# A Fourier mixing layer and MLP: the first stage of two sequences in stacked form, and Silu in one pass

## Chip, core and metric

The kernel runs on one core of one Trainium2 chip. The metric is the device time of one execution in microseconds. The core's engines are named as in the profile: PE (TensorE matmul), PEld (its weight load), ACT (ScalarE), DVE (VectorE), POOL (GpSimd) and SP (SyncE, which here only issues DMAs).

## What is computed

`x` holds 4 sequences of 3008 tokens with 256 features. Each goes through a real Fourier transform over the tokens, a complex 256 x 256 product with a soft threshold, and the inverse transform; an MLP with 2048 hidden features and SiLU follows.

```python
X = rfft(x, axis=1)
Yr = Xr @ w_r - Xi @ w_i + b_r
Yi = Xr @ w_i + Xi @ w_r + b_i
Y = sign(Y) * maximum(abs(Y) - 0.01, 0)     # Yr and Yi apart
y = irfft(Y, n=3008, axis=1).reshape(12032, 256)
h = y @ w_in
out = (h / (1 + exp(-h))) @ w_out
```

## The kernel before

**The transform.** 3008 = 47 x 64: token t = 64 n2 + n1, with n2 below 47 and n1 = 32 h + j (h is 0 or 1, j below 32). The first stage ("s1") sums over n2 for 24 residues r, real and imaginary part: a product with a small table of cosines and sines. It writes to a scratch tensor in HBM (`scr1`). The second part works in 12 units `u` of two residues: `u_load` reads a unit back, `s2` or `s2_3` does the other DFT, `mix` or `mix3` the complex product, the threshold follows (in `mix3` as `shrink`, put off to the next tick), `i1` does the first inverse step and writes `scr2`. The last inverse step `i2` reads `scr2` through `g_load` and leaves y, transposed, in SBUF for the MLP.

**The MLP** goes through 24 blocks of 512 tokens (the last has 256) with 16 hidden slices `f` each, 376 pairs (i, f). One pair is a "tick". In tick t PE does `mlp1` of pair t (line 499, 6 matmuls of 512 columns), then what the tick has been given besides ("fill"), then `mlp2` of pair t-2 (lines 539 and 543). Between them ACT takes the sigmoid of h from PSUM (line 506), DVE multiplies it by h (line 507); one tick later `split_g` rounds g to the part gh on ACT (line 516) and leaves the rest gl to DVE (line 517).

**Split numbers.** A matmul in fp32r rounds its operands, so a value goes in as a high part and a rest, and a product is high x high + high x rest + rest x high: three matmuls (`s1_product`, line 173).

**What sets the order.** The code is written out tick by tick; each engine runs its own instructions in that order. Sequence 0 is transformed ahead of the ticks (prologue), with part of sequence 1's first stage and the split of the first MLP weights. `fill` holds the rest: `at` puts a call in a tick, `put` in the next tick that is not taken. `W_GO` says how many steps of the weights' split (`w64_split`, lines 599 to 613, on ACT and DVE in turn) go into ticks 0 to 22. `mix3_weights` makes wi - wr and wi + wr and their splits with POOL (lines 315 and 319). `x_ahead` issues the next load of x on POOL's queue (line 158, 94 rows of 4 KB). Stores go through a list that `flush` issues on SP's queue.

**First stage of sequences 2 and 3** (b = 2, 3). A group g of 4 token columns (of 8) is a tile of 94 rows, (n2, h). `s1_split` rounds one half of it, 512 columns, on ACT (line 218) and subtracts on DVE (line 219); in a later tick `s1_half` multiplies (line 173, three matmuls), copies the result on ACT and splits the other half. That is 16 halves a sequence and 3 matmuls a half.

**End of the prologue** (lines 738 to 763). The last `i1` of sequence 0 stores to `scr2` through ACT's queue (line 138). `g_load` of groups 0 and 1 for rows 0 to 87, a store of sequence 1's first stage (`flush(1)`), and `g_load` for rows 88 to 95, which waits for that last store, follow on SP; then `i2(0, 0)` can run. Block 0 needs columns j = 0 to 5, that is group 0 and the first half of group 1.

Of the kernel before, what the change touches and what calls it, by code (L numbers as in the profile page):

```python
# [37 lines left out]
def dft_tables():  # L38

    n1 = np.arange(KK)  # L40
    n2 = np.arange(RR)
    r = np.arange(NR)
    k = np.arange(KK)

    def trig(num, den):
        num = np.mod(num, den)
        c, s = np.cos(2 * np.pi * num / den), np.sin(2 * np.pi * num / den)
        s = np.where(2 * num % den == 0, 0.0, s)
        return c, s
# [48 lines left out]


@with_exitstack  # L100
def spectral_mlp_kernel(ctx: ExitStack, tc: tile.TileContext, x, w_r, w_i, b_r, b_i, w_in, w_out, c1, c2, c3, c4, c3f, out):
    nc = tc.nc
    cst = ctx.enter_context(tc.tile_pool(name="cst", bufs=1))
    sb = ctx.enter_context(tc.tile_pool(name="sb", bufs=2))
# [18 lines left out]
    def bank(name):  # L123

        tag, bufs = "d", 2
        if state["prologue"]:
            state["d"] = (state["d"] + 1) % 4
            tag, bufs = (("d", 2), ("acc", 4), ("h", 2), ("acc", 4))[state["d"]]
        return ps.tile([128, 512], F32, tag=tag, bufs=bufs, name=name)
# [28 lines left out]
            nc.gpsimd.dma_start(out=t[:NP, :], in_=v)  # L158
        return t

    x_next = [(b, g) for b in range(NB) for g in range(8)]

    def x_ahead():
        if x_next:
            q = x_next.pop(0)
            x_t[q] = x_load(*q)

    x_t = {}
    x_pre = []
# [42 lines left out]
            store(v[:, g * 4 * D:(g + 1) * 4 * D], o)  # L212
            del x_t[1, g], x_t[1, g, "o"]

    def s1_split(b, g, i):
        t = x_t[b, g][:NP, i * 512:(i + 1) * 512]
        sx = sb.tile([128, 2, 512], F32R, tag="sx", bufs=1, name="sx")
        nc.scalar.copy(sx[:NP, 0, :], t)
        nc.vector.tensor_sub(sx[:NP, 1, :], t, sx[:NP, 0, :])  # L219
        x_t[b, g, i] = sx  # L220

    def s1_half(b, g, i):
        sx = x_t.pop((b, g, i))
        if i == 0:
            x_t[b, g, "o"] = sb.tile([128, 4 * D], F32, tag="s1o", bufs=2, name="s1o")[:96, :]
        o = x_t[b, g, "o"]
        p = bank("s1")
        s1_product(p, (sx[:, 0, :], sx[:, 1, :]))
        nc.scalar.copy(o[:, i * 512:(i + 1) * 512], p[:96, :])
        if i == 0:  # L230
            s1_split(b, g, 1)
        else:
            v = scr1[b].rearrange("r (a j) d -> (r a) (j d)", a=4)
            store(v[:, g * 4 * D:(g + 1) * 4 * D], o)
            del x_t[b, g], x_t[b, g, "o"]
            x_ahead()
# [68 lines left out]
    def mix3_weights():  # L305
        t = sb.tile([128, 2, 2 * D], F32, tag="s1o", bufs=2, name="w32")
        nc.sync.dma_start(out=t[:, :, 0:D], in_=w_r.rearrange("(e p) d -> p e d", p=128))
        nc.sync.dma_start(out=t[:, :, D:2 * D], in_=w_i.rearrange("(e p) d -> p e d", p=128))
        for i, v in enumerate((b_r, b_i)):
            nc.sync.dma_start(out=bias[:, i, :], in_=v.unsqueeze(0).to_broadcast([128, D]))  # L310
        yield
        ds = []
        for op in (ALU.subtract, ALU.add):
            ds.append(sb.tile([128, 2, D], F32, tag="i1o", bufs=2, name="w32d"))
            nc.gpsimd.tensor_tensor(out=ds[-1], in0=t[:, :, D:2 * D], in1=t[:, :, 0:D], op=op)
        yield
        for d, dst in zip(ds, (wi, ws)):
            nc.scalar.copy(dst[0], d)
            nc.gpsimd.tensor_sub(dst[1], d, dst[0])

    def s2_3(b, u):
        a, t2 = u_t[b, u]
# [83 lines left out]

    g_t = {}

    def g_load(b, g, rows=slice(0, 96)):

        if (b, g) not in g_t:
            g_t[b, g] = sb.tile([96, 4 * D], F32, tag="gin", bufs=4, name="gin")
        v = scr2[b].rearrange("r (a j) d -> (r a) (j d)", a=4)
        nc.sync.dma_start(out=g_t[b, g][rows, :], in_=v[rows, g * 4 * D:(g + 1) * 4 * D])

    def pieces(c0, n):

# [74 lines left out]
    def mlp1(i, f):  # L492
        n = BLOCKS[i][1]
        h, l = xt[i]
        p = ps.tile([128, 512], F32, tag="h", bufs=2, name="h")
        m = 0
        for e in range(2):
            for w, v in ((win[0], h), (win[1], h), (win[0], l)):
                nc.tensor.matmul(  # L499
                    out=p[:, :n], lhsT=w[:, e, f * 128:(f + 1) * 128], rhs=v[:, e, :n],  # L500
                    start=(m == 0), stop=(m == 5),
                )
                m += 1
# [111 lines left out]
    with tc.manual_schedule():  # L615
        first = sb.tile([128, 1], F32, tag="rest", bufs=1, name="first")
        nc.gpsimd.memset(first, 0.0)
        nc.scalar.activation(out=first, in_=first, func=ACTF.Sigmoid)
        zero = sb.tile([128, 512], F32, tag="c", bufs=1, name="zero")
        x_sb.append(sb.tile([128, 4 * D], F32, tag="sx", bufs=1, name="x_sb2"))  # L620
        x_pre.extend(x_sb)
# [127 lines left out]
        w_go()
        w_tags[:] = [(("zl", 2), ("zh", 2))]  # L750
# [107 lines left out]
```

## Time and profile before

| | |
|---|---|
| runs | 1384.2 us median of 3 (1383.86 to 1386.02) |
| profiled execution | 1384.09 us, span of its instructions 1382.2 us |
| busy | PE 1362.8 us (99%), PEld 1166.1 (84%), DVE 887.7 (64%), ACT 704.8 (51%), POOL 98.6 (7%) |
| mean granted TensorE clock | 0.997 |
| DMA | 103.51 MB, 75 GB/s over the span |

A busy share counts an engine's instructions from start to end, and matmuls overlap, so 99% on PE says that it seldom sat without one, not that it ran at its peak. The chain that ended last goes back from the last instruction to what released it. The timeline shows single instructions, with the wait ahead of one and its releaser in brackets.

### The profile page before, as it was taken

The numbers are of one execution on the slowest core, as the hardware profiler recorded it, in microseconds if no ns is written. First come the engines' busy times: TensorE is split into PE (matmuls) and PEld (weight loads), VectorE is DVE, ScalarE is ACT, GpSimd is POOL, SyncE is SP. The second block draws the span as 40 slices with busy tenths as digits, with TensorE's granted clock in tenths as the row PEclk, the third lists the DMA queues.
The fourth block names the chain that finished last, engine by engine and source line by source line (L and its number), as shares of the span: only waits on it lengthen the run. The fifth ranks groups of instructions, "written<-read, shape, count | busy, mean of one in ns | idle before, by whom it ended". The sixth has DMA issues, their size and how long they took to land.

```text
span 1382.2 us, 20362 instructions
## 1 busy us (share of the span) xinstructions
PE 1362.8 (99%) x7621; PEld 1166.1 (84%) x7621; DVE 887.7 (64%) x1517; ACT 704.8 (51%) x1386; POOL 98.6 (7%) x145
## 2 busy tenths in 40 slices
PE   8989999999999999999999999999999999999998
PEld 4967788888888888888888888888888888888888
DVE  3858969687655677767655577776654555455555
ACT  5545455555564555555454445454454444444444
POOL 2000012111100101111100011111000000000000
PEclk9999999999999999999999999999999999999999
DMA  8865314231423213333121022220210110011001
GB/s 283 260 214 157 113 55 119 70 102 32 121 77 102 58 42 107 86 98 80 47 76 53 21 77 59 76 81 24 61 29 15 27 39 10 18 27 39 0 16 24
DMA packets 69939, 103.51 MB, mean 75 GB/s; under 512 B 7313, under 2 KB 53009, under 8 KB 69841
## 3 DMA queue, kind: packets, MB, share of 16 engines
q1 hardware_dynamic: 58169, 79.07, 19.6%
q0 software_dynamic: 8096, 19.45, 5.2%
q10 hardware_dynamic: 3575, 3.70, 0.9%
q8 instruction: 60, 0.98, 0.3%
q14 instruction: 39, 0.31, 0.1%
HBM read 64.70 MB, written 37.49 MB: 74 GB/s over the span
## 4 chain that ended last, share of the span: by engine, by line
PE 92%; DVE 3%; DMA 2%; ACT 1%; issue 1%; SPq 0%; DVEq 0%; ACTq 0%
PE h L499 36%; PE acc L539 24%; PE acc L543 12%; PE mix L352 5%; PE i L442 3%; PE mix L291 2%; PE s L327 2%; PE i L400 2%; PE s L173 2%; PE acc L534 1%; DMA scr<-s1o 1%; PE i L397 1%; PE s L270 1%; PE i2e L442 1%; DVE gl L517 1%
## 5 line engine op out<-in xcount | busy, mean ns | idle before, releaser
L499 PE MATMUL h<-xt,win 128*128 128x512 f32 (+1 forms) x2304 | 584.8, 389 | 0.0
L539 PE MATMUL acc<-wout,gh 128*128 128x512 f32 x1472 | 540.4, 401 | 0.7 <-ACT gh L516 0.7
L499 PEld LDWEIGHTS h<-xt,win 128*128 128x128 f32 x2304 | 400.9, 188 | 82.2 <-DVE xt L459 0.4
L506 ACT ACTIVATE g<-h 128x512 f32<-128x512 f32 (+1 forms) x385 | 226.4, 588 | 378.4 <-PE h L499 377.4
L543 PE MATMUL acc<-wout,gl 128*128 128x256 f32 x1472 | 412.8, 280 | 3.4 <-DVE gl L517 3.3
L507 DVE TENSOR_TENSOR g<-h,g 128x512 f32<-128x512 f32 (+1 forms) x385 | 261.2, 678 | 236.7 <-ACT g L506 233.0
L517 DVE TENSOR_TENSOR gl<-g,gh 128x512 fp32r<-128x512 f32 (+1 forms) x385 | 276.4, 718 | 172.5 <-ACT gh L516 167.3
L539 PEld LDWEIGHTS acc<-wout,gh 128*128 128x128 f32 x1472 | 276.9, 188 | 61.6 <-ACT gh L516 2.4
L516 ACT CAST gh<-g 128x512 fp32r<-128x512 f32 (+1 forms) x385 | 235.1, 611 | 155.2 <-DVE g L507 152.7
L543 PEld LDWEIGHTS acc<-wout,gl 128*128 128x128 f32 x1472 | 278.0, 189 | 15.2 <-DVE gl L517 6.0
L359 POOL TENSOR_TENSOR q<-q,bias 128x256 f32<-128x256 f32 x36 | 26.4, 733 | 652.5 <-ACT q L358 652.5
L442 PEld LDWEIGHTS i<-c_sb,gin 96*128 96x128 f32 x420 | 55.5, 195 | 11.3 <-issue 5.8
L372 DVE TENSOR_TENSOR y<-q,mix 64x256 f32<-64x256 f32 x144 | 60.3, 419 | 2.2
L442 PE MATMUL i<-c_sb,gin 96*128 96x94 f32 x420 | 54.7, 275 | 5.6 <-DMA gin<-scr 5.6
L327 PEld LDWEIGHTS s<-t,a 128*128 128x128 f32 x288 | 37.7, 191 | 3.0
L327 PE MATMUL s<-t,a 128*128 128x128 f32 x288 | 37.9, 274 | 0.0
L459 DVE TENSOR_TENSOR xt<-i,xt 128x376 fp32r<-128x376 f32 (+2 forms) x48 | 28.0, 584 | 14.7 <-ACT xt L458 14.7
L173 PE MATMUL s<-sx,c 94*96 94x512 f32 (+1 forms) x111 | 34.1, 414 | 0.3 <-DVE sx L219 0.3
L458 ACT CAST xt<-i 128x376 fp32r<-128x376 f32 (+2 forms) x48 | 24.2, 503 | 19.9 <-PE i L442 19.9
L400 PE MATMUL i<-zh,t 128*128 128x256 f32 x144 | 33.7, 297 | 0.0
L404 ACT COPY i1o<-i 128x512 f32<-128x512 f32 x48 | 27.9, 581 | 9.5 <-PE i L397 8.2
L560 DVE TENSOR_TENSOR o<-acc,o 128x256 f32<-128x256 f32 x92 | 32.6, 414 | 0.0
(119 smaller groups left out, 1168.8 us busy)
## 6 DMA issues: line engine op xcount, KB each, us to landing
a<-scr SPq DMA_DIRECT2D x48, 256.0 KB
gin<-scr SPq DMA_DIRECT2D x30, 384.0 KB
scr<-s1o SPq DMA_DIRECT2D x29, 384.0 KB
t<-in_c_dram POOLq DMA_DIRECT2D x36, 256.0 KB, 3.0
scr<-i1o SPq DMA_DIRECT2D x36, 256.0 KB
x_sb<-in_x_dram POOLq DMA_DIRECT2D x22, 376.0 KB, 4.2
t<-in_c_dram SPq DMA_DIRECT2D x48, 128.0 KB
w<-in_moe_w_in_dram SPq DMA_DIRECT2D x8, 512.0 KB
```

What stands on the lines that cost most here:

```text
L173: nc.tensor.matmul(out=p[:96, :], lhsT=c1_hl[m][:K, :], rhs=hl[k][:K, :], start=(n == 0), stop=(n == 2))
L327: nc.tensor.matmul(out=pv[:, e, :, r, :], lhsT=a[:, r, e * 128:(e + 1) * 128], rhs=t2[:, r * 128:(r + 1) * 128], start=True, stop=True,)
L352: nc.tensor.matmul(out=out, lhsT=x_[:, e, c, :], rhs=m[:, e, :], start=(n == 0), stop=(n == 5))
L400: nc.tensor.matmul(out=pv[:, r, :], lhsT=t3[:, m, q], rhs=z[k][:, r, :], start=(n == 0), stop=(n == 2),)
L442: nc.tensor.matmul(out=p[:, o:o + m], lhsT=g_t[b, j // 4][:, q:q + 128], rhs=c4_sb[:, p0:p0 + m], start=True, stop=True,)
L499: nc.tensor.matmul(out=p[:, :n], lhsT=w[:, e, f * 128:(f + 1) * 128], rhs=v[:, e, :n], start=(m == 0), stop=(m == 5),)
L506: nc.scalar.activation(out=g[:, q], in_=p[:, q], func=ACTF.Sigmoid)
L507: nc.vector.tensor_tensor(out=g[:, q], in0=p[:, q], in1=g[:, q], op=ALU.mult)
L516: nc.scalar.copy(gh[:, q], g[:, q])
L517: nc.vector.tensor_sub(gl[:, q], g[:, q], gh[:, q])
L539: nc.tensor.matmul(out=a, lhsT=gh[:, q], rhs=wout[:, f].rearrange("p a c -> p (a c)"), start=begins, stop=False,)
L543: nc.tensor.matmul(out=a[:, D:2 * D], lhsT=gl[:, q], rhs=wout[:, f, 0, :], start=False, stop=ends,)
```

## The change

Four things change.

1. *First stage of sequences 2 and 3, stacked.* A piece q (16 a sequence) takes one half h of n1 and 4 columns j. `x_load_twice` loads its 47 rows of 1024 columns twice, to partitions 0 to 46 and 64 to 110 of one tile (two DMAs on POOL's queue). `stack_split` rounds all 111 partitions in one ACT pass and turns the second copy into the rest on DVE. A new table `c5` holds the high part of the cosines and sines in 64 output columns and the rest in the other 64. `stack_product` then needs one matmul for 512 columns, two a piece; ACT copies the lower output half out of PSUM and DVE adds the upper one. The product comes two ticks after the split, not one.
2. *Silu in one ACT pass* in place of Sigmoid on ACT and a multiply on DVE.
3. *`mix3_weights` on DVE* instead of POOL, its last two steps in ticks 22 and 23 instead of 19 and 22.
4. *End of the prologue*: only the first half of group 1 is loaded ahead of `i2(0, 0)`; its other half, and the first-stage store, follow behind the loads of rows 88 to 95.

The ticks of the first stage and of the units of sequences 2 and 3 move with it.

```diff
+    c, s = trig(np.outer(n2, r), RR)
+    c5 = np.zeros((128, 2, KK))
+    c5[:RR, 0, :2 * NR] = np.stack([c, -s], axis=2).reshape(RR, 2 * NR)
...
+    c5[:RR, 1] = c5[:RR, 0] - c5h
+    c5[:RR, 0] = c5h
+    c5[64:64 + RR] = c5[:RR]
...
+    def x_load_twice(b, q):
+        t = x_sb[q % 2]
+        if b == STACKED and q < 2:
+            nc.gpsimd.memset(t[32:64, :], 0.0)
+        h, g = divmod(q, 8)
+        v = x[b].rearrange("(n h j) d -> n h (j d)", h=2, j=NJ)[:, h, g * 4 * D:(g + 1) * 4 * D]
+        for p in (0, 64):
+            nc.gpsimd.dma_start(out=t[p:p + RR, :], in_=v)
+        return t
...
-    def s1_split(b, g, i):
...
-    def s1_half(b, g, i):
...
+    def stack_split(b, q):
+        t = x_t[b, q]
+        sx = sb.tile([128, 4 * D], F32R, tag="sx", bufs=1, name="sx")
+        nc.scalar.copy(sx[:64 + RR, :], t[:64 + RR, :])
+        nc.vector.tensor_sub(sx[64:64 + RR, :], t[64:64 + RR, :], sx[64:64 + RR, :])
+        x_t[b, q] = sx
+
+    def stack_product(b, q):
+        sx = x_t.pop((b, q))
+        o = sb.tile([128, 4 * D], F32, tag="s1o", bufs=2, name="s1o")[:2 * NR, :]
+        for i in range(2):
+            p = bank("s1")
+            c = slice(i * 512, (i + 1) * 512)
+            nc.tensor.matmul(out=p, lhsT=c5_sb[:64 + RR, :], rhs=sx[:64 + RR, c], start=True, stop=True)
+            nc.scalar.copy(o[:, c], p[64:64 + 2 * NR, :])
+            nc.vector.tensor_tensor(out=o[:, c], in0=p[:2 * NR, :], in1=o[:, c], op=ALU.add)
...
+        x_ahead()
...
-            nc.gpsimd.tensor_tensor(out=ds[-1], in0=t[:, :, D:2 * D], in1=t[:, :, 0:D], op=op)
+            nc.vector.tensor_tensor(out=ds[-1], in0=t[:, :, D:2 * D], in1=t[:, :, 0:D], op=op)
...
-            nc.gpsimd.tensor_sub(dst[1], d, dst[0])
+            nc.vector.tensor_sub(dst[1], d, dst[0])
...
-            nc.scalar.activation(out=g[:, q], in_=p[:, q], func=ACTF.Sigmoid)
-            nc.vector.tensor_tensor(out=g[:, q], in0=p[:, q], in1=g[:, q], op=ALU.mult)
+            nc.scalar.activation(out=g[:, q], in_=p[:, q], func=ACTF.Silu)
...
+        urgent = (slice(0, 4 * D), slice(0, 2 * D))
         for g in range(2):
             loaded.add((0, g))
-            g_load(0, g, slice(0, 88))
-        flush(1)
+            g_load(0, g, slice(0, 88), urgent[g])
         u_step(NU + 1)
         s1(1, 3, late=True)
         for g in range(2):
-            g_load(0, g, slice(88, 96))
+            g_load(0, g, slice(88, 96), urgent[g])
+        flush(1)
+        g_load(0, 1, cols=slice(2 * D, 4 * D))
...
-        for t in (16, 19, 22):
+        for t in (16, 22, 23):
             at(t, next, m3, None)
...
-        for b, t0, dt in ((1, t + 11, 3.1), (2, 92, 5), (3, 186, 5)):
+        for b, t0, dt in ((1, t + 11, 3.1), (2, 104, 4.3), (3, 190, 4.8)):
...
-        for b, t0, dt in ((2, 37, 6), (3, 110, 8)):
+        for b, t0, dt in ((2, 54, 2.8), (3, 114, 4.4)):
             t = 0
-            for g in range(8):
-                t = max(t, t0 + dt * g)
-                at(t, s1_split, b, g, 0)
-                t = put(t + 1, s1_half, b, g, 0)
-                t = put(t + 1, s1_half, b, g, 1)
+            for q in range(16):
+                t = max(t, int(t0 + dt * q))
+                at(t, stack_split, b, q)
+                t = put(t + 2, stack_product, b, q)
```

**Where instructions move.** PE, in sequence 2's first stage, around one product (`s` is a PSUM bank, `c` the table, `sx` the split x). Before, one half:

```order
L499 MATMUL h<-xt_3309,win_79 128x512
L173 MATMUL s_3936<-sx,c_0_67 96x512 x2
L173 MATMUL s_3936<-sx,c_1_68 96x512
L539 MATMUL acc<-wout,gh 128x512
L543 MATMUL acc<-wout,gl 128x256
```

Now, one piece:

```order
L523 MATMUL h<-xt_3230,win_80 128x512
L254 MATMUL s_3974<-sx,c_sb 128x512
L254 MATMUL s_3978<-sx,c_sb 128x512
L562 MATMUL acc<-wout,gh 128x512
L566 MATMUL acc<-wout,gl 128x256
```

Three matmuls a half become two a piece, on another table.

ACT in the same stage, from one product to the next thing it copies out, before:

```order
L229 COPY s1o<-s_3775 96x512
L218 CAST sx<-x_sb_70 94x512
L516 CAST gh<-g 128x512
L506 ACTIVATE g<-h 128x512
L229 COPY s1o<-s_3808 96x512
```

And now:

```order
L255 COPY s1o<-s_3844 48x512
L255 COPY s1o<-s_3848 48x512
L244 CAST sx<-x_sb_70 111x1024
L539 CAST gh<-g 128x512
L530 ACTIVATE g<-h 128x512
L482 CAST xt_3813<-i_3879 128x376
```

A tick with a product holds two copies of 48 x 512 and a split of 111 x 1024, and the next tick none of them.

SP at the end of the prologue (`gin` is what `g_load` fills, `scr1_1` takes the first stage of sequence 1). Before:

```order
L414 DMA gin_967<-scr2_0_86 88x1024
L414 DMA gin_969<-scr2_0_86 88x1024
L142 DMA scr1_1_83<-s1o_960 96x1024
L414 DMA gin_967<-scr2_0_86 8x1024
L414 DMA gin_969<-scr2_0_86 8x1024
L583 DMA w64_999<-in_moe_w_out_dram 128x2x512
```

And now:

```order
L438 DMA gin_968<-scr2_0_87 88x1024
L438 DMA gin_970<-scr2_0_87 88x512
L438 DMA gin_968<-scr2_0_87 8x1024
L438 DMA gin_970<-scr2_0_87 8x512
L157 DMA scr1_1_84<-s1o_961 96x1024
L438 DMA gin_970<-scr2_0_87 96x512
L606 DMA w64_1001<-in_moe_w_out_dram 128x2x512
```

The store stood ahead of the loads of the last 8 rows and stands behind them; the second load is half as wide.

DVE during the split of the weights (`ww` and `we`), ticks 2 to 4, before:

```order
L601 TENSOR_SCALAR ww<-ww 128x512
L602 SCALAR_TENSOR_TENSOR ww<-w_1055,ww 128x512
L517 TENSOR_TENSOR gl<-g,gh 128x512
L507 TENSOR_TENSOR g<-h,g 128x512
L459 TENSOR_TENSOR xt_1090<-i_1150,xt_1089 128x376
L608 TENSOR_SCALAR we<-ww 128x512
L609 SCALAR_TENSOR_TENSOR we<-w_1055,we 128x512
L612 TENSOR_TENSOR ww<-ww,win_79 128x512
L613 TENSOR_TENSOR win_80<-ww,we 128x512
```

And now:

```order
L624 TENSOR_SCALAR ww<-ww 128x512
L625 SCALAR_TENSOR_TENSOR ww<-w_1057,ww 128x512
L540 TENSOR_TENSOR gl<-g,gh 128x512
L483 TENSOR_TENSOR xt_1090<-i_1148,xt_1089 128x376
L631 TENSOR_SCALAR we<-ww 128x512
L632 SCALAR_TENSOR_TENSOR we<-w_1057,we 128x512
L635 TENSOR_TENSOR ww<-ww,win_80 128x512
L636 TENSOR_TENSOR win_81<-ww,we 128x512
```

The multiply `g<-h,g` is gone from between gl and the weights' steps.

## Rows read from the trace of the kernel before

**Rows 1.** Page, part 4: the chain that ended last, by engine.

```profile
PE 92%; DVE 3%; DMA 2%; ACT 1%; issue 1%; SPq 0%; DVEq 0%; ACTq 0%
```

**Rows 2.** Stretches: length, busy PE, PEld, DVE, ACT, POOL, clock, DMA share, GB/s.

```profile
80.00:100.00 20.00, 15.31 (x68) 10.21 (x67) 9.83 (x17) 8.40 (x15) 0.00 (x0) 0.92 0.63 205
...
160.00:180.00 20.00, 17.52 (x83) 13.73 (x84) 18.39 (x29) 9.78 (x19) 1.23 (x2) 1.00 0.30 86
...
400.00:500.00 100.00, 100.00 (x552) 85.98 (x550) 61.26 (x104) 51.44 (x99) 6.10 (x10) 1.00 0.24 71
```

**Rows 3.** Chain in order (start us, us, what), two pairs of ticks.

```profile
176.39 1.39 PE h L499 x6
179.17 1.39 PE h L499 x6
...
399.35 1.39 PE h L499 x6
402.83 1.39 PE h L499 x6
```

**Rows 4.** Groups by shape: busy us, mean ns, idle before, its releasers.

```profile
L507 DVE TENSOR_TENSOR g<-h,g 128x512 f32<-128x512 f32 x368 | 254.3, 691 | 234.1 <-ACT g L506 231.9
...
L506 ACT ACTIVATE g<-h 128x512 f32<-128x512 f32 x368 | 220.0, 598 | 374.9 <-PE h L499 374.6
...
L219 DVE TENSOR_TENSOR sx<-x_sb,sx 94x512 fp32r<-94x512 f32 x32 | 22.4, 699 | 10.0 <-ACT sx L218 9.9
...
L608 DVE TENSOR_SCALAR we<-ww 128x512 uint32<-128x512 uint32 x16 | 7.8, 487 | 0.3
```

**Rows 5.** Timeline 88 to 104 us: start us, us, what, wait.

```profile
88.03 0.72 SPq L414 DMA_DIRECT2D gin<-scr  x2
...
88.45 0.41 ACTq L138 DMA_DIRECT2D scr<-i1o  x1
...
88.84 0.31 SPq L142 DMA_DIRECT2D scr<-s1o  x1
...
95.50 0.60 SPq L414 DMA_DIRECT2D gin<-scr  x2
...
97.64 2.42 PE L442 MATMUL i<-c_sb,gin 96*128 96x94 f32 x10 [4.69 <-DMA gin<-scr]
...
103.80 1.25 PE L442 MATMUL i<-c_sb,gin 96*128 96x94 f32 x10
```

**Rows 6.** Short stretches, columns as in rows 2.

```profile
30.00:32.00 2.00, 0.98 (x9) 1.01 (x10) 0.69 (x1) 0.97 (x3) 0.00 (x0) 1.00 0.97 289
...
96.00:97.00 1.00, 0.00 (x0) 0.00 (x0) 0.00 (x0) 0.00 (x0) 0.00 (x0) 0.85 0.24 66
...
103.00:104.00 1.00, 1.00 (x5) 0.54 (x3) 0.10 (x1) 0.25 (x1) 0.00 (x0) 0.74 0.00 0
```

**Rows 7.** Timeline of ticks 0 to 24, columns as in rows 5.

```profile
104.83 3.42 PE L499 MATMUL h<-xt,win 128*128 128x512 f32 x12
...
109.64 0.68 PE L442 MATMUL i<-c_sb,gin 96*128 96x94 f32 x4 [0.96 <-DMA gin<-scr]
...
125.87 1.02 PE L208 MATMUL s<-x_sb,c_sb 128*96 128x512 f32 x2
...
158.28 2.71 POOL L315 TENSOR_TENSOR w32d<-w 128x512 f32<-128x512 f32 x2 [26.92 <-DMA w<-in_w_i_dram]
...
158.45 1.42 DVE L608 TENSOR_SCALAR we<-ww 128x512 uint32<-128x512 uint32 x1
...
162.20 0.38 PE L543 MATMUL acc<-wout,gl 128*128 128x256 f32 x1 [1.50 <-DVE gl L517]
...
181.78 1.55 PE L499 MATMUL h<-xt,win 128*128 128x512 f32 x6
```

**Rows 8.** Line 158's transfers; the stretch 8 to 10 us as in rows 2.

```profile
DMA to landing us min/median/max: 3.4/4.5/9.5
...
8.00:10.00 2.00, 1.67 (x5) 0.73 (x5) 0.00 (x0) 1.02 (x2) 0.52 (x1) 1.00 1.02 272
```

More of the change, by code (lines that the diff above doesn't have):

```diff
@@ L32 @@
 S1_SPLIT = (3, 4, 5, 6, 7)
+STACKED = 2
 X_BUFS = [0, 1, 2, 3, 4, 5, 6, 0, 1, 2, 3, 4, 0, 2, 1, 0]
@@ L90, in dft_tables @@
     c3f = c3
+    c, s = trig(np.outer(n2, r), RR)
+    c5 = np.zeros((128, 2, KK))
+    c5[:RR, 0, :2 * NR] = np.stack([c, -s], axis=2).reshape(RR, 2 * NR)
+    c5[:, :, 1] = 0.0
+    c5 = c5.astype(np.float32)
+    bits = c5[:RR, 0].view(np.uint32).astype(np.uint64)
+    c5h = ((bits + 0x7FF + ((bits >> 12) & 1)) & 0xFFFFF000).astype(np.uint32).view(np.float32)
+    c5[:RR, 1] = c5[:RR, 0] - c5h
+    c5[:RR, 0] = c5h
+    c5[64:64 + RR] = c5[:RR]
     return {
@@ L96, in dft_tables, with spectral_mlp_kernel @@
         "c3f": c3f,
+        "c5": c5.reshape(128, 128),
     }
 @with_exitstack
-def spectral_mlp_kernel(ctx: ExitStack, tc: tile.TileContext, x, w_r, w_i, b_r, b_i, w_in, w_out, c1, c2, c3, c4, c3f, out):
+def spectral_mlp_kernel(ctx: ExitStack, tc: tile.TileContext, x, w_r, w_i, b_r, b_i, w_in, w_out, c1, c2, c3, c4, c3f, c5, out):
     nc = tc.nc
@@ L111, in spectral_mlp_kernel @@
     c4_sb = cst.tile([96, NP], F32, name="c4_sb")
+    c5_sb = cst.tile([128, 128], F32R, name="c5_sb")
     bias = cst.tile([128, 2, D], F32, name="bias")
@@ L159, in x_load @@
         return t
-    x_next = [(b, g) for b in range(NB) for g in range(8)]
+    def x_load_twice(b, q):
[7 more added lines that the diff above has]
+        return t
+    x_next = [(b, g) for b in range(NB) for g in range(16 if b >= STACKED else 8)]
     def x_ahead():
@@ L165, in x_ahead @@
             q = x_next.pop(0)
-            x_t[q] = x_load(*q)
+            x_t[q] = (x_load_twice if q[0] >= STACKED else x_load)(*q)
     x_t = {}
@@ L213, in s1_later @@
             del x_t[1, g], x_t[1, g, "o"]
-    def s1_split(b, g, i):
[L216 to L220, printed above, removed]
-    def s1_half(b, g, i):
[L223 to L236, printed above, removed]
+    def stack_split(b, q):
[13 more added lines that the diff above has]
+            nc.vector.tensor_tensor(out=o[:, c], in0=p[:2 * NR, :], in1=o[:, c], op=ALU.add)
+        h, g = divmod(q, 8)
+        v = scr1[b].rearrange("r (i h j) d -> (r i) h (j d)", i=2, h=2)
+        store(v[:, h, g * 4 * D:(g + 1) * 4 * D], o)
+        x_ahead()
     u_t = {}
@@ L407, in spectral_mlp_kernel, with g_load @@
     g_t = {}
-    def g_load(b, g, rows=slice(0, 96)):
+    def g_load(b, g, rows=slice(0, 96), cols=slice(0, 4 * D)):
         if (b, g) not in g_t:
             g_t[b, g] = sb.tile([96, 4 * D], F32, tag="gin", bufs=4, name="gin")
-        v = scr2[b].rearrange("r (a j) d -> (r a) (j d)", a=4)
-        nc.sync.dma_start(out=g_t[b, g][rows, :], in_=v[rows, g * 4 * D:(g + 1) * 4 * D])
+        v = scr2[b].rearrange("r (a j) d -> (r a) (j d)", a=4)[:, g * 4 * D:(g + 1) * 4 * D]
+        nc.sync.dma_start(out=g_t[b, g][rows, cols], in_=v[rows, cols])
     def pieces(c0, n):
@@ L617, in spectral_mlp_kernel @@
         nc.gpsimd.memset(first, 0.0)
-        nc.scalar.activation(out=first, in_=first, func=ACTF.Sigmoid)
+        nc.scalar.activation(out=first, in_=first, func=ACTF.Silu)
         zero = sb.tile([128, 512], F32, tag="c", bufs=1, name="zero")
@@ L796, in spectral_mlp_kernel @@
             at(t, x_ahead)
+        at(30, nc.gpsimd.dma_start, c5_sb, c5)
         m3 = mix3_weights()
-        for t in (16, 19, 22):
+        for t in (16, 22, 23):
             at(t, next, m3, None)
         t = 13
-        for b, t0, dt in ((1, t + 11, 3.1), (2, 92, 5), (3, 186, 5)):
+        for b, t0, dt in ((1, t + 11, 3.1), (2, 104, 4.3), (3, 190, 4.8)):
             at(t0 - 2, u_load, b, 0)
```

## Prediction

> **What bounds the kernel now.** I read the chain that ended last first, because it says which engine the end hangs on: PE holds 92% of it [rows 1]. Next come the stretches, which say where PE does not run: from 400 to 500 us it is busy for all 100, with DVE at 61 and ACT at 51; from 80 to 100 us it is busy for 15.31 of 20, from 160 to 180 us for 17.52 [rows 2]. In the second of these DVE is busy for 18.39 of 20, which 400 to 500 us is far from. So outside the first 182 us only less work on PE shortens the kernel; inside them there are waits to win. Last I read starts of ticks, since "busy" also counts a matmul that stands and waits: a plain tick lasts 179.17 - 176.39 = 2.78 us, a tick with a first-stage half 402.83 - 399.35 = 3.48 [rows 3]. Six matmuls of 512 columns take 1.39 us there, 0.232 each.
>
> **The sum** is made against the profiled execution, 1384.1 us; the median of the runs is 1384.2, so I add nothing for that.
>
> *Stacked first stage.* Removed are 32 halves of 0.70 us (3.48 - 2.78), 22.4 us. Added are 64 matmuls of 512 columns. No row has one of 111 rows and 128 output columns; the first MLP layer with 128 and 128 takes 0.232, the old half with 94 and 96 took 0.70 / 3 = 0.233 [rows 3], so size between these does not matter: 64 x 0.232 = 14.8 us. Term: **-7.6 us**, all on the path, since PE does not wait in that stage.
>
> Around it ACT and DVE get more for a piece. On ACT: two copies of 48 x 512 and a split of 111 x 1024. On DVE: two adds and a subtraction of 47 x 1024. Copies cost about the 0.60 of an ACT pass over 512 columns, adds 0.69 to 0.70 [rows 4]; the 1024 wide ones cost at most twice the 512 wide, 1.2 and 1.4. A tick with a product then asks ACT for its usual two passes and 2.4 us more, 3.6, against 2.78 + 0.46 = 3.24 on PE, and its neighbour without one for 1.2 against 2.78: 4.8 of 6.0 in two ticks. DVE gets 2.8 more a piece and loses 0.69 a tick. What PE needs in a tick was rounded in the tick before, so a late ACT in one of two has over a us to make it good: nothing on the path. If that cover is gone, see the third rival.
>
> On POOL's queue 64 loads of 47 rows take the place of 16 of 94, on SP's 32 stores of half the size that of 16; the bytes read for x double. The old loads land in 4.5 us (median) [rows 8]. A buffer is free once its split is done (1.2 + 1.4 us), then the next load is issued (two DMAs, about 0.5 us apart) and must land before the split two pieces on: 2.6 + 0.5 + 4.5 = 7.6 us in a time of four ticks and four matmuls, 12.0 us. So 4.4 us of slack, and nothing on the path.
>
> For these loads a rule of the Trainium skill speaks against the change. The page "DMA: Bandwidth & Descriptors", section "Why a DMA increments its semaphore by 16 and not by 1", says that a DMA runs on the largest number of engines, up to 16, that divides its row count, which leaves 47 rows one engine and 94 rows two; it knows an exception, some POOL-issued copies that get ceil(rows / 16) rows an engine on 16. Rows 8 disagree with the rule and agree with the exception: 385 kB in 4.5 us is 86 GB/s, and two engines at the 17 GB/s that one moves in the stretch shown (272 / 16) would need 11.3 us. By the rule the sum would be that of the last rival.
>
> *End of the prologue.* PE stands for 4.69 us until `gin` lands at 97.64. The loads of the last 8 rows leave SP at 95.50, 7.05 us after the store that they wait for, at 88.45 [rows 5]. In its way on the DMA engines are two loads of 88 rows, 704 KB, and, issued at 88.84, a store of 384 KB; with its own 256 KB that is 1376 kB in 7.05 us, 195 GB/s, and the stretch has 205 [rows 2]. So it waits for bytes. Now 352 + 176 + 256 KB = 803 kB stand there, 4.1 us. If the order counts more than the bytes, only the 176 KB go, 0.9 us. Ends: -0.9 and -2.9; I take -2.2, as the three share the engines to the end. Term: **-2.2 us**. Late next is the store itself, issued some 5 us later, whose buffer a later first-stage copy of the prologue needs; several steps of PE lie between.
>
> *Clock.* The granted clock fell to 1.2 GHz at about 96.7 (0.85 in that us), after 3.7 us without a matmul, and was back at 2.4 GHz at about 103.5 (0.74 in that us); where PE was idle half the time, at 30 to 32 us, it stayed at 1.00 [rows 6]. An idle time of 2.5 us lies between; I take the clock to stay, as the fall came well after that much. Ten `i2` matmuls took 2.42 us at the low level and 1.25 at the high one [rows 5]; PE worked 5.9 us at the low level, so 2.9 us come back at most and 0 at least. Some of that turns into waits on ACT: **-2.0 us**.
>
> *Silu, and POOL's work on DVE.* From the first `mlp1` at 104.83 to tick 24 at 181.78 [rows 7] are 76.95 us. Work for PE in it: 24 ticks x 2.78 = 66.7, less 2.8 (two ticks have no `mlp2`), plus 20 `i2` matmuls at 0.125, 2.5, plus two late first-stage products of 1.02 [rows 5, 7]: 68.4. So 8.5 us are waits. 1.0 is for `gin` [rows 7] and stays. 1.9 come with POOL's two passes at 158.28: beside them line 608 takes 1.42 us where its mean is 0.49 [rows 4, 7], and the next DVE step is as late again; PE then waits 1.50 for gl. With this work on DVE they go; four passes of 0.69 come to DVE in ticks 22 and 23, which is not full there. The other 5.6 come from DVE's order: the multiply (0.69 us) stands ahead of the weights' steps, waits for the sigmoid, and ACT waits for those steps before it rounds the next g. Without it DVE falls from 18.39 to about 13.5 of 20 us. I take two thirds, 3.7. An ACT pass with Silu is not in the trace; it lies between the 0.60 of Sigmoid [rows 4] and that plus the multiply, and I take 0.60, the same engine and tile. The new order has a single load of a function table, as before. Ends: -1.9 and -7.5. Term: **-5.6 us**. In the remaining 1200 us 254 us of DVE work go and buy nothing, since PE is busy there throughout.
>
> *Ticks of units and pieces moved.* The same work on PE in other ticks; sequence 2's units end by tick 164 where its first block is loaded at 167, sequence 3's by 258 for 263. Nothing.
>
> Sum: -7.6 - 2.2 - 2.0 - 5.6 = -17.4, so 1366.7; **I say 1366.5 us**, its own range 1361 to 1370.
>
> **Rivals.**
> - *The prologue keeps its gap* (14%): the store's 7 us are its own latency, and the clock falls as before. Against it speaks 195 GB/s beside 205. 4.2 us less: 1370.7.
> - *The weights still hold ticks 0 to 23* (10%): ACT and DVE take turns over the weights as before, and only POOL's 1.9 us come back. For it: the steps wait for each other, not only for the multiply. 1370.4.
> - *Both product banks in one tick* (11%): a product now takes both rotating PSUM banks at once, and waits for the pass that reads the older one, or ACT is late with its 3.6 us. At 0.25 us a tick in 32 ticks it is 8 us: 1374.5; at 0.55, as much as the 17 us won, it is no change. Against it: two ticks lie between products.
> - *One engine for 47 rows* (5%): if a load of 47 rows goes through a single DMA engine, 192.5 kB at 17 GB/s [rows 8] are 11.3 us; with the 3.1 us that are left of 4.5 after 385 kB at 272 GB/s, a load lands in 14.4. The loop of split, issue and load is then 17.5 us against 12.0, and ACT stands in front of its split with Silu queued behind it. 5.5 us in each of seven pairs of sequence 2, 38 us: 1405, slower. It decides for slower from a landing of 11.5 us on; sequence 3, with pieces 4.4 ticks apart, is spared. Against it speak the 86 GB/s of the loads of 94 rows. This is what the Trainium skill's rule above would do.
>
> **How the numbers follow.** Forecast 60%, rivals 14, 10, 11 and 5%. The range 1361 to 1374.5 takes in the forecast, the first two rivals and most of the third; left out are the third's upper part (5%), the last (5%) and a gain over 23 us (6%). Within 0.2%, 2.8 us, a measurement of this kernel can't be told from no change. Faster by more: the forecast, the first two, 8 of the third's 11 and 1 of the last's 5, together 93%; the same 3%; slower 4%.
>
> **What would show it.** Right: 15 + 64 matmuls in the first stage's split form, product ticks of 3.24 us; `i2(0, 0)` some 2 us after PE stops rather than 4.69, at the high clock; from first `mlp1` to tick 24 about 71 us; DVE near 690 us in all; x landing below 6 us. Wrong: product ticks over 3.4 us; ACT waiting for x in the split; DVE still near 18 of 20 us during the weights; a clock below 1.00 between 90 and 105 us.

## The result, and the profile after

| | before | after |
|---|---|---|
| runs | 1384.99 us median of 4 (1383.86 to 1386.02) | 1367.85 us median of 4 (1367.0 to 1368.81) |
| profiled execution, span | 1384.09, 1382.2 us | 1368.02, 1366.0 us |
| busy PE, DVE, ACT, POOL | 1362.8, 887.7, 704.8, 98.6 us | 1352.8, 686.1, 727.9, 126.0 us |

The ratio of the times is 0.987 (95% interval 0.9856 to 0.9884): faster by 17 us.

The page after, first the chain that ended last by engine, as in [rows 1], then the first-stage pass of DVE and the DMA group of x (last number: median us from issue to landing):

```profile
PE 96%; DMA 3%; ACT 1%; issue 0%; DVE 0%; SPq 0%; ACTq 0%
...
L245 DVE TENSOR_TENSOR sx<-x_sb,sx 47x1024 fp32r<-47x1024 f32 x32 | 40.7, 1271 | 22.3 <-ACT sx L244 21.4
...
x_sb<-in_x_dram POOLq DMA_DIRECT2D x64, 188.0 KB, 3.5
```

DVE has left the chain (3% in [rows 1]). The 47-row loads land in 3.5 us, sooner than the 94-row ones [rows 8]. The stretches of [rows 2], columns as there:

```profile
80.00:100.00 20.00, 17.31 (x92) 12.22 (x91) 11.97 (x21) 9.91 (x20) 0.00 (x0) 0.99 0.62 188
160.00:180.00 20.00, 20.00 (x106) 16.98 (x105) 12.79 (x22) 10.65 (x21) 0.00 (x0) 1.00 0.18 54
...
400.00:500.00 100.00, 100.00 (x543) 85.99 (x543) 51.77 (x85) 59.73 (x113) 10.02 (x18) 1.00 0.33 88
```

From 160 to 180 us PE now runs throughout, and DVE, at 18.39 of 20 before, is at 12.79. The chain in order of time, a plain tick and one with a stacked product:

```profile
171.92 1.39 PE h L523 x6
174.71 1.38 PE h L523 x6
...
344.00 1.38 PE h L523 x6
345.38 0.47 PE s L254 x2
347.24 1.39 PE h L523 x6
```

2.79 us, and 347.24 - 344.00 = 3.24. All 32 product ticks take 3.2 or 3.3 us, and from 174 us to the end PE has no wait for another engine. The end of the prologue, answering to [rows 5]:

```profile
90.81 6.28 SPq L438 DMA_DIRECT2D gin<-scr  x4
...
91.30 0.38 ACTq L153 DMA_DIRECT2D scr<-i1o  x1
...
92.20 3.60 PE L218 MATMUL s<-x_sb,c_sb 128*96 128x512 f32 x8
98.48 1.45 PE L466 MATMUL i<-c_sb,gin 96*128 96x94 f32 x10 [2.69 <-DMA gin<-scr]
99.73 1.92 PE L234 MATMUL s<-x_sb,c_sb 128*96 128x512 f32 x2
```

The wait for `gin` is 2.69 us instead of 4.69. But the clock fell again; short stretches:

```profile
98.00:99.00 1.00, 0.52 (x5) 0.55 (x5) 0.00 (x0) 0.00 (x0) 0.00 (x0) 1.00 1.13 270
99.00:100.00 1.00, 1.00 (x9) 1.00 (x8) 0.00 (x0) 0.03 (x1) 0.00 (x0) 0.77 0.93 264
100.00:101.00 1.00, 1.00 (x2) 0.35 (x2) 0.45 (x1) 0.52 (x1) 0.00 (x0) 0.50 0.64 148
...
102.00:103.00 1.00, 1.00 (x4) 0.52 (x3) 0.25 (x1) 0.49 (x2) 0.00 (x0) 0.52 1.04 397
103.00:104.00 1.00, 1.00 (x8) 0.73 (x6) 0.00 (x0) 0.59 (x2) 0.00 (x0) 1.00 0.96 391
```

It fell at about 99.5, when PE had been working again for a us, and was at 2.4 GHz again from 103.0: 3.4 us at 1.2 GHz, where the kernel before has 6.8 (96.7 to 103.5).

**The balance** is read in four parts, which the later runs use too. *Lead*: up to the end of the last early first-stage product (before 89.78 + 3.17 = 92.95, after 92.20 + 3.60 = 95.80). *Gap*: from there to the first `mlp1` (104.83 in [rows 7]; 104.49). *Weights*: from there to tick 24 (181.78; 174.54). *Rest*: to the end of the span.

| us | lead | gap | weights | rest | span |
|---|---|---|---|---|---|
| before | 92.95 | 11.88 | 76.95 | 1200.4 | 1382.2 |
| after | 95.80 | 8.69 | 70.05 | 1191.5 | 1366.0 |
| difference | +2.85 | -3.19 | -6.90 | -8.9 | -16.2 |

The lead grew by 2.85 us in code that the change hardly touches. Whether the change does that, or whether executions differ there by themselves, was the first question for the runs.

### The profile page after: what moved, and what is told of

It is laid out like the page before. It is cut to its first block, busy times and chain, and to the rows that moved or that the text cites. A ratio compares the mean times of both kernels' runs of the same rounds, so it can differ in the third digit from the quotient of the medians.

```text
span 1366.0 us, 20164 instructions
## 1 busy us (share of the span) xinstructions
PE 1352.8 (99%) x7589; PEld 1163.0 (85%) x7589; DVE 686.1 (50%) x1200; ACT 727.9 (53%) x1418; POOL 126.0 (9%) x192
## 4 chain that ended last, share of the span: by engine, by line
PE 96%; DMA 3%; ACT 1%; issue 0%; DVE 0%; SPq 0%; ACTq 0%
PE h L523 38%; PE acc L562 25%; PE acc L566 13%; PE mix L376 6%; PE i L466 3%; PE s L351 2%; PE i L424 2%; PE mix L315 2%; PE s L254 1%; DMA scr<-i1o 1%; PE acc L557 1%; DMA scr<-s1o 1%; PE i2e L466 1%; PE i L421 1%; PE s L218 1%; PE s L294 1%
## 5 line engine op out<-in xcount | busy, mean ns | idle before, releaser
L540 DVE TENSOR_TENSOR gl<-g,gh 128x512 fp32r<-128x512 f32 (+1 forms) x385 | 264.6, 689 | 349.9 <-ACT gh L539 348.2
L383 POOL TENSOR_TENSOR q<-q,bias 128x256 f32<-128x256 f32 x36 | 26.4, 734 | 592.8 <-ACT q L382 592.8
L256 DVE TENSOR_TENSOR s1o<-s,s1o 48x512 f32<-48x512 f32 x64 | 41.0, 678 | 48.2 <-ACT s1o L255 46.5
L245 DVE TENSOR_TENSOR sx<-x_sb,sx 47x1024 fp32r<-47x1024 f32 x32 | 40.7, 1271 | 22.3 <-ACT sx L244 21.4
L361 DVE TENSOR_TENSOR xs<-s,xs 128x256 f32<-128x256 f32 x36 | 15.3, 424 | 70.9 <-ACT xs L360 70.9
L184 POOL DMA_DIRECT2D x_sb<-in_x_dram x64 | 32.8, 514 | 142.4 <-ACT sx L244 125.4
L384 POOL TENSOR_TENSOR q<-q,bias 128x256 f32<-128x256 f32 x36 | 37.5, 1042 | 2.8
```

The costliest lines, as they stand in the source:

```text
L245: nc.vector.tensor_sub(sx[64:64 + RR, :], t[64:64 + RR, :], sx[64:64 + RR, :])
L256: nc.vector.tensor_tensor(out=o[:, c], in0=p[:2 * NR, :], in1=o[:, c], op=ALU.add)
L540: nc.vector.tensor_sub(gl[:, q], g[:, q], gh[:, q])
```

## One part at a time

Four kernels, each the one before with a single part of the change, timed together against 1385.8 us (median of 19 runs of the kernel before). Their edits are pieces of the diff above; the only one not to be cut out by lines is the first, which keeps the moved ticks:

```diff
 only_stacked: the diff without its Silu, mix3_weights and g_load pieces
 only_silu:
-            nc.scalar.activation(out=g[:, q], in_=p[:, q], func=ACTF.Sigmoid)
-            nc.vector.tensor_tensor(out=g[:, q], in0=p[:, q], in1=g[:, q], op=ALU.mult)
+            nc.scalar.activation(out=g[:, q], in_=p[:, q], func=ACTF.Silu)
 only_dve_weights:
-            nc.gpsimd.tensor_tensor(out=ds[-1], in0=t[:, :, D:2 * D], in1=t[:, :, 0:D], op=op)
+            nc.vector.tensor_tensor(out=ds[-1], in0=t[:, :, D:2 * D], in1=t[:, :, 0:D], op=op)
 (the two subtractions alike, and the ticks 16, 22, 23)
 only_prologue: the g_load pieces, urgent and flush(1)
```

**Stacked first stage.**

> The stacked first stage and the moved ticks alone: Sigmoid with its multiply, POOL's part of the weights and the old order of the prologue's end stay. My theory: 64 matmuls of 0.232 us for 96 make 7.6 us, with up to 1.5 more because a tick's waits elsewhere go too, so 1375 to 1377 us. First mlp1 to tick 24 stays at about 77 us, product ticks last 3.24 us. Rival (products need both banks at once and are only hidden by the DVE that Silu freed): product ticks of over 3.4 us, 1380 us or more.

**Silu.**

> The kernel before with Silu in one ScalarE pass in place of Sigmoid and a multiply on DVE. My theory: DVE's order held the weights' ticks, so first mlp1 to tick 24 falls from 77 us to 72 to 73.5, POOL's two passes still cost about 1.9, the rest of the kernel does not change: 1380 to 1381 us. Rival (the weights' steps wait for each other, not for the multiply): within 1 us of the kernel before, the stretch at 76 us or more.

**POOL's work on DVE.**

> The kernel before with POOL's four passes over the mix weights on DVE, in the new ticks, the multiply left on DVE. My theory: the 1.9 us that come with POOL's passes go, but four passes of 0.69 us come to a DVE that is full in these ticks, so 1382.3 to 1384, the stretch from first mlp1 to tick 24 at 75 to 77 us. Rival (POOL's passes were the main cause of the waits): 1379 or less.

**Order of the prologue's loads.**

> The kernel before with the new order of loads at the end of the prologue and nothing else. My theory: the wait ahead of the first i2 falls from 4.69 to about 2.7 us, the granted clock still falls but for about half as long, so from the end of the last early first-stage matmul to the first mlp1 3.2 us less: 1380.5 to 1381.5 us. Rival (what is won there is lost further up the prologue by the change itself, as the first mlp1 of the changed kernel came only 0.3 us earlier): the kernel before within 0.7 us, and again waits of some 2.9 us between 10 and 90 us that the kernel before has not.

| | median us | ratio, 95% interval | lead | gap | weights | rest |
|---|---|---|---|---|---|---|
| only_stacked | 1378.87 | 0.9949 (0.9933 to 0.9965) | 94.71 | 11.11 | 76.90 | 1193.2 |
| only_silu | 1379.07 | 0.9943 (0.9931 to 0.9955) | 96.13 | 11.71 | 70.02 | 1199.6 |
| only_dve_weights | 1384.05 | 0.9987 (0.9977 to 0.9997) | 93.85 | 12.37 | 75.70 | 1200.5 |
| only_prologue | 1382.11 | 0.997 (0.9959 to 0.9981) | 94.64 | 8.72 | 77.00 | 1200.4 |

Each part moved the stretch that it should, by 1.25 to 7.2 us; the other stretches, the lead apart, moved by at most 0.8 us. Whole runs, up to 7.6 us apart for one kernel, show this less clearly. In `only_silu` and `only_dve_weights` nothing ahead of the gap is changed but the first activation's function in the one, and their leads are 96.13 and 93.85: the lead varies by itself, and the 2.85 us need no effect of the change. `only_prologue`'s rival falls: its median lies 3.7 us under that of the kernel before, not within 0.7, and its gap is the 8.7 us of the whole change.

The stacked stage is worth 1200.4 - 1193.2 = 7.2 us, near the expectation. Its median was above what was expected, but so was that of the kernel before, 1385.8. Two of its 32 product ticks take 3.55 us, the others 3.2 or 3.3, so the rival's ticks of over 3.4 us came in two of 32 and cost 0.6 us.

Silu gave more than either theory said: the weights went from 76.95 to 70.02 us, all that the whole change gets there, **with POOL's passes still on POOL**. In the kernel before `mlp2` waits for ACT and DVE, and nearly all of that lies in this stretch (groups of the whole span: busy, mean ns, idle before, its releasers):

```profile
L539 PE MATMUL acc<-wout,gh 128*128 128x512 f32 x1472 | 540.4, 401 | 0.7 <-ACT gh L516 0.7
...
L543 PE MATMUL acc<-wout,gl 128*128 128x256 f32 x1472 | 412.8, 280 | 3.4 <-DVE gl L517 3.3
```

In `only_silu` it has neither wait. These are 4.0 of the 6.9 us; the other 2.9 come off the time that counts as busy on PE (71.88 to 68.97 us), in which a matmul can also stand and wait. How POOL's delay disappears is to be read from DVE's rows, groups of the stretch 105 to 182 us in `only_silu` (busy, mean ns, idle before, its releasers):

```profile
L516 DVE TENSOR_TENSOR gl<-g,gh 128x512 fp32r<-128x512 f32 x24 | 17.1, 713 | 12.2 <-ACT gh L515 12.1
...
L611 DVE TENSOR_TENSOR ww<-ww,wout 128x512 f32<-128x512 f32 x6 | 4.1, 684 | 0.0
L611 DVE TENSOR_TENSOR ww<-ww,win 128x512 f32<-128x512 f32 x4 | 3.8, 960 | 0.0
```

and in the kernel before:

```profile
L517 DVE TENSOR_TENSOR gl<-g,gh 128x512 fp32r<-128x512 f32 x23 | 16.0, 695 | 5.6 <-ACT gh L516 4.6 <-PE h L499 1.0
```

DVE is still held up while POOL works: of the four steps with a mean of 960 ns three take 0.69 us as their like do, and the one beside POOL's second pass takes 1.78, 1.1 more. But DVE now idles for 12.2 us ahead of `gl` in that stretch, not 5.6, which is room for such a delay; that it costs nothing there is what `no_dve_weights` below shows. Silu takes the multiply out of DVE's order and also out of the way from h to `gh`. Which of the two frees the weights' ticks no run here tells apart.

`only_dve_weights` came out as its theory has it, with a median 1.75 us under that of the kernel before: the 1.50 us wait at tick 16 [rows 7] is gone, the weights are 1.25 us shorter, and the smaller waits for `gl` and `gh` stay.

## Taking parts away from the changed kernel

Four more, each the changed kernel with one edit, against 1385.56 us (9 runs of the kernel before).

```diff
 no_silu: Sigmoid and the multiply back
 no_dve_weights: gpsimd back in the four passes, ticks 16, 19, 22
 one_tick:
-                t = put(t + 2, stack_product, b, q)
+                t = put(t + 1, stack_product, b, q)
 fill_gap, ahead of i2(0, 0):
+        p = bank("warm")
+        for i in range(2):
+            nc.tensor.matmul(out=p[:96, :], lhsT=c1_sb, rhs=x_t[1, 6][:, i * 512:(i + 1) * 512], start=True, stop=True)
```

> The changed kernel with Sigmoid and the multiply on DVE put back. My theory: the stretch from first mlp1 to tick 24 goes from 70.05 back to the 75.7 us that the run with the weights on DVE alone showed, and 0.8 us come at the end, where the last ticks have nothing beside them: 6 to 7 us more than the changed kernel, 1373.5 to 1375. Rival (Silu is needed to pay for the stacked first stage, whose adds and wide subtraction load DVE): product ticks over 3.4 us and 1377 or more.

> The changed kernel with the four passes over the mix weights back on POOL, in the old ticks 16, 19, 22. Silu alone had the stretch from first mlp1 to tick 24 at 70.02 us, as short as with both. My new theory: POOL's passes cost only in a DVE order that the multiply fills, so the stretch stays at 70.0 to 70.3 us and the time within 1.5 us of the changed kernel. Rival (my prediction's step: 1.9 us are POOL's own): 72 us, 1369.7.

> The changed kernel with a piece's product one tick after its split instead of two. Theory: ACT has its two passes, the split of 1.2 us and then in the next tick two copies more; a product in a tick right behind its split can find DVE's subtraction late, at most 0.3 us a tick in those of the 32 where the placement makes a difference: 0 to 5 us more. Rival (the second tick is needed): product ticks over 3.4 us throughout and 8 us or more.

> The changed kernel with two products more between the last early first-stage product and the first i2: the x tile of piece 6 times the first-stage table, 4 bytes, 512 columns, about 0.96 us each, their results never read. They lie in the 2.69 us in which PE waits for gin. My theory: the granted clock stays at 2.4 GHz, and i2 and the late products between there and the first mlp1 take 3.9 us instead of 5.8; part turns into waits on ACT, so 0.7 to 1.9 us less than the changed kernel, 1366 to 1367.2. Rival (ACT's and DVE's steps there set the pace): the clock stays up and the time is within 0.4 us. Second rival: the clock falls all the same.

| | median us | ratio, 95% interval | lead | gap | weights | rest |
|---|---|---|---|---|---|---|
| no_silu | 1375.41 | 0.9927 (0.9914 to 0.9939) | 97.82 | 9.02 | 75.65 | 1193.2 |
| no_dve_weights | 1368.69 | 0.988 (0.9866 to 0.9893) | 95.38 | 10.53 | 70.44 | 1191.8 |
| one_tick | 1378.4 | 0.9953 (0.994 to 0.9967) | 92.30 | 9.01 | 70.52 | 1204.0 |
| fill_gap | 1365.99 | 0.9861 (0.9847 to 0.9874) | 93.06 | 7.22 | 70.72 | 1191.4 |

*Without Silu* the median is some 7.6 us above that of the changed kernel, a little more than expected: the weights are back at 75.65 us, the number that the theory took from `only_dve_weights`, and the rest is 1.7 longer, not 0.8. Compared tick by tick, that is 0.6 at tick 35, 0.3 in each of two product ticks (3.56 us for 3.26 and 3.23) and 0.3 behind the last `mlp1`. Silu is not what carries the stacked stage.

*Without DVE's passes* nothing changes that the runs can tell (0.988 beside 0.987), and the weights stay 0.4 us from the changed kernel. Beside Silu this part of the change buys nothing: the rival, my prediction's step, falls.

*One tick* costs 10.6 us against the changed kernel by the medians and 12.5 in the rest. My theory, 5 us at most, falls. The rival's 8 us or more came, though not in every product tick: 17 of the 32 take 3.6 to 4.8 us, the other 15 are as they were. Who waited for whom in it, from tick 25 on (us in total, times, longest):

```profile
PE s L254 <- DVE sx L245: 5.3, 12, 0.8
PE s L254 <- DVE y L396: 2.6, 2, 1.3
```

and its DVE rows around one such tick (start us, us, wait):

```profile
354.61 1.28 DVE L256 TENSOR_TENSOR s1o<-s,s1o 48x512 f32<-48x512 f32 x2 [0.55 <-ACT s1o L255]
356.05 1.22 DVE L245 TENSOR_TENSOR sx<-x_sb,sx 47x1024 fp32r<-47x1024 f32 x1 [0.15 <-ACT sx L244]
357.30 0.69 DVE L540 TENSOR_TENSOR gl<-g,gh 128x512 fp32r<-128x512 f32 x1
```

The adds of one piece stand ahead of the split of the next, the split ends at 357.27, and the product waits for it. With two ticks the split has a tick in between, and in the changed kernel no product waits.

*Filling the gap*: PE's wait ahead of `i2` is 1.18 us, the clock stays at 2.4 GHz over the whole stretch, and the gap is 7.22 us, 1.5 less than in the changed kernel. In the timed runs, beside 0.987, this is not told apart.

```profile
90.00:106.00 16.00, 13.28 (x59) 7.80 (x57) 6.99 (x13) 8.91 (x18) 0.00 (x0) 1.00 0.76 245
```

## A version that might beat both, and the loads on another queue

The last four share a chip, with the kernel before at 1386.79 us (9 runs).

```diff
 changed_again: the changed kernel
 work_ahead:
-        i2(0, 0)
         s1_later(6, 0)
-        i2_ends(0)
         s1_later(6, 1)
+        i2(0, 0)
+        i2_ends(0)
         i2(0, 1)
 one_ahead:
-        i2(0, 0)
         s1_later(6, 0)
-        i2_ends(0)
+        i2(0, 0)
         s1_later(6, 1)
+        i2_ends(0)
         i2(0, 1)
 sp_loads:
-            nc.gpsimd.dma_start(out=t[p:p + RR, :], in_=v)
+            nc.sync.dma_start(out=t[p:p + RR, :], in_=v)
```

> The changed kernel itself, beside the three others on the same chip. All theories: ratio 0.986 to 0.988 to the kernel before. What it tells: how far its prologue up to the first mlp1, which no part of the change touches until the last loads, varies by itself; in the profiles so far the last early first-stage product ended anywhere from 92.3 to 97.8 us.

> The changed kernel with both late products of piece 6 moved ahead of the first i2: the same work, in the gap in which PE waits for gin. Two products that were thrown away there kept the granted clock at 2.4 GHz and gave 1.5 us. My theory: the clock stays up here too, and 2.06 us of products come off the path besides; i2 then follows i2 with nothing between, which gives back up to 1 us as a wait for ACT and DVE: 2 to 3.5 us less than the changed kernel, 1364.3 to 1366. Rival (the wait for the next gin, 1.32 us long behind the first mlp1, grows by what is won): 0.5 us less at most.

> The changed kernel with only the first of the two late products of piece 6 moved ahead of the first i2, and the second between i2 and its ends. PE then idles about 1.7 us there, between the 1.18 us at which the granted clock stayed and the 2.69 us at which it fell. Theory A: the clock stays; 1.03 us of work come off the path and 1.5 us for the clock, no wait is added: 2 to 2.8 us less than the changed kernel, 1365 to 1366. Theory B: the clock falls as in the changed kernel: 0.5 to 1.2 us less.

> The changed kernel with the 64 loads of 47 rows of x issued by SP in place of POOL. In the changed kernel they land in 3.5 us. My theory: the rows are spread over the engines whoever issues them: they land within 5 us and the time stays within 2 us of the changed kernel. Rival (the Trainium skill, page DMA: Bandwidth & Descriptors, section Why a DMA increments its semaphore by 16 and not by 1: one engine for 47 rows, and its exception is for copies that POOL issues): a load lands in 11 us or more, product ticks wait for x in sequence 2, 1390 us or more.

| | median us (range) | ratio, 95% interval | lead | gap | weights | rest |
|---|---|---|---|---|---|---|
| changed_again | 1366.76 (1366.17 to 1368.07) | 0.9859 (0.9845 to 0.9872) | 93.76 | 8.80 | 70.58 | 1191.4 |
| work_ahead | 1365.21 (1365.01 to 1365.8) | 0.9847 (0.9834 to 0.986) | 94.79 | 7.22 | 70.25 | 1191.4 |
| one_ahead | 1366.33 (1364.44 to 1367.39) | 0.9854 (0.984 to 0.9867) | 94.55 | 8.00 | 69.67 | 1191.4 |
| sp_loads | 1589.88 (1588.38 to 1591.51) | 1.1467 (1.1451 to 1.1483) | 95.82 | 10.39 | 70.31 | 1413.2 |

*changed_again* repeats the changed kernel's time. Its lead is 93.76 us where the same code had 95.80, and its weights are 0.5 us longer; the rest is the same within 0.1.

*work_ahead* gave less than I expected, 1.55 us, though its four runs all lie below all four of the changed kernel. Its timeline and clock:

```profile
97.49 1.32 PE L466 MATMUL i<-c_sb,gin 96*128 96x94 f32 x10 [0.99 <-DMA gin<-scr]
98.65 0.61 PE L466 MATMUL i2e<-c_sb,gin 96*128 96x94 f32 x4
99.10 1.75 PE L466 MATMUL i<-c_sb,gin 96*128 96x94 f32 x10
102.01 5.21 PE L523 MATMUL h<-xt,win 128*128 128x512 f32 x12 [1.16 <-ACT xt L500]
```

```profile
98.00:99.00 1.00, 1.00 (x12) 1.00 (x10) 0.00 (x0) 0.00 (x0) 0.00 (x0) 1.00 0.86 254
99.00:100.00 1.00, 1.00 (x11) 1.00 (x9) 0.00 (x0) 0.31 (x1) 0.00 (x0) 0.87 0.95 219
100.00:101.00 1.00, 0.85 (x4) 0.61 (x3) 0.00 (x0) 0.76 (x2) 0.00 (x0) 0.50 0.92 297
```

The clock fell at about 99.7, after a wait of only 0.99 us and two us of `i2`, and twelve matmuls of `mlp1` took 5.21 us where the kernel before has 3.42 [rows 7]; PE also waited 1.16 us for ACT. So the 2.06 us of products came off the path and 1.55 us were won; what a clock that stays would have added did not come. *one_ahead*: the clock fell too, as theory B has it, at about 99.0 after a wait of 1.93 us, and 0.4 us were won, just under its lower end. Of all kernels here `work_ahead` is the fastest, 0.1% under the changed one; a version that takes its order and keeps the clock up was not tried.

*sp_loads* is the surprise. With the other engine issuing the same loads the time is 223 us longer. Its chain, three pieces in order of time (start us, us, what), SP's issues of two pieces of x, and a stretch:

```profile
403.18 27.59 DMA x_sb<-in_x_dram
...
433.36 27.58 DMA x_sb<-in_x_dram
...
463.52 27.59 DMA x_sb<-in_x_dram
```

```profile
402.87 7.25 SPq L184 DMA_DIRECT2D x_sb<-in_x_dram  x2
...
417.34 8.48 SPq L184 DMA_DIRECT2D x_sb<-in_x_dram  x2
```

```profile
420.00:430.00 10.00, 7.41 (x33) 5.97 (x31) 1.36 (x2) 0.59 (x1) 0.00 (x0) 0.84 0.06 27
```

The DMA engines are 0.06 busy, one of sixteen, and move 27 GB/s. At that rate the two loads of a piece, 385 kB, take 14.3 us, and the pieces do follow each other about every 15 us, where the changed kernel has one about every 6. A load lands 27.6 us after its issue, as the piece before it is still being loaded then. Issued by POOL each lands in 3.5 us. The late pieces are not all of it: PE waits 80.7 us in products for the split, but also 51.8 us for `gin` (4.0 in the changed kernel), whose loads stand on SP's queue too.

```profile
PE s L254 <- DVE sx L245: 80.7, 12, 15.8
...
PE i L466 <- DMA gin<-scr: 51.8, 7, 17.6
```

My theory falls. The rule in the Trainium skill, page "DMA: Bandwidth & Descriptors", section "Why a DMA increments its semaphore by 16 and not by 1", that 47 rows leave one engine, agrees with this run for the loads that SP issues; its exception for POOL's copies agrees with the changed kernel.

## Why the prediction was right, point by point

It was right in sign and size: 1366.5 us said, 1367.85 measured. By term it was less exact: the weights gave 1.3 us more than said and the rest too, the gap 1.0 less. The parts sum to -19.0, not -17.4, and came out as -16.2 in the profiled pair because of the lead, which varies by itself. So that the total came within 1.4 us is in part luck.

- **Stacked first stage, said -7.6.** Alone it is -7.2; on top of Silu 1199.6 - 1191.5 = -8.1, since 0.6 of waits in two product ticks go with the multiply. Its basis, 0.232 us for a matmul of this shape, holds: the chain has 0.47 for two. ACT's and DVE's load stayed off the path. The second load of a piece is mostly issued 1.25 us after the first, not 0.5, which the slack covers. And the run with one tick shows that this rests on the two ticks: without that cover it costs 10.6 us.
- **End of the prologue, said -2.2.** The wait went from 4.69 to 2.69: -2.0. The last loads leave SP 5.2 us after the store (91.30 to 96.49), not 7.05 as in [rows 5]. So the first rival (14%), in which the 7 us are the store's own, falls, though the clock fell as it says; with bytes alone it would have been 4.1.
- **Clock, said -2.0.** This step failed: "I take the clock to stay, as the fall came well after that much". With 2.69 us of wait it fell, and in the other six kernels with this order and nothing put into the gap, with 2.73 to 3.01 us, it fell too. The gap as a whole is -3.2 for a predicted -4.2, so with 2.0 from the wait the clock gave about -1.2: the low level lasted 3.4 us, not 6.8. That is not sure to come: in `no_dve_weights` and `sp_loads`, with the same code up to the first `mlp1`, it lasted 6.8 us, and the gaps are 10.53 and 10.39.
- **Silu, and POOL's work on DVE, said -5.6.** -6.9. That the multiply held the weights' ticks was right (the second rival, 10%, falls with `only_silu`) and the two thirds too careful: about all 5.6 us went. The division was wrong. I gave POOL's passes 1.9 us of their own; alone they are worth 1.25, and beside Silu nothing.
- **"In the remaining 1200 us 254 us of DVE work go and buy nothing"**: they buy 0.8 us alone (1200.4 to 1199.6) and 1.7 in the changed kernel (1193.2 to 1191.5).
- **Third rival (11%)**, both banks in one tick: no product waits at two ticks in the changed kernel. **Fourth (5%)**, one engine for 47 rows: it did not happen because POOL issues them. Had it happened, the 38 us that I gave it were far too few, as the 223 us of `sp_loads` show. One engine moved 27 GB/s there and not 17, but I let the two loads of a piece run side by side, and on one engine they follow each other: 15 us a piece in place of 17.5 for two. `sp_loads` is not quite that rival either, since its loads share SP's queue with those of `gin`.

- **The lead**, of which the prediction did not speak, is 2.85 us longer in the profiled execution after than in the one before. Leads with the old order of loads are 92.95, 93.85, 94.71 and 96.13, with the new one 92.30 to 97.82 (10 profiles): executions differ by more than the two orders do. A part of the longest, 97.82 in `no_silu`, is the clock, at 0.50 there from 34 to 37 us; what makes the others differ stays open.

## What to carry to other kernels

Split the span at marks that every variant has, and compare the parts: here parts of 1 to 7 us behind the prologue stood out clear, while whole runs of one kernel differed by up to 7.6 us. A stretch that differs between executions of the same code, as the lead and the gap do here, needs several profiles. When two edits both relieve one engine, run each alone and both together before giving each its own term: here one of them was worth 1.25 us alone and nothing beside the other. And the price of a transfer can hang on the engine that issues it, so read the landing time for that very shape and engine.

## What the runs showed of the hardware that I had not expected

- 47 rows of 4 KB land in 3.5 us when POOL issues the load. When SP does, they move at 27 GB/s with the DMA engines 0.06 busy, about 15 us for two loads, and land 27.6 us after their issue with the piece before them still under way.
- The granted clock can fall while PE works: at 99.5 us in the changed kernel, a us after its matmuls had begun again, and in `work_ahead` after a wait of 0.99 us and over two us of matmuls of 94 columns. In `fill_gap`, with a wait of 1.18 us between first-stage products and `i2`, it stayed at 2.4 GHz. So the longest wait alone does not tell whether it falls; what does stays open, with one profile of each.
- A Silu pass of ACT over 128 x 512 takes just what a Sigmoid pass takes in [rows 4], so the multiply came off for nothing. The group by shape, after:

```profile
L530 ACT ACTIVATE g<-h 128x512 f32<-128x512 f32 x368 | 220.0, 598 | 500.9 <-PE h L523 499.0
```
